# Sliding-window attention and mixture of experts on one core: attention's order written anew, four pairs' softmax sums moved to VectorE

## The chip, the core and the metric

One core of a Trainium2 chip runs the whole program in one launch. The metric is the device time in microseconds (us) of the program; lower is better. Engines are named as in the profile: PE (TensorE matmul), PEld (its weight loads), DVE (VectorE), ACT (ScalarE), POOL (GpSimd), SP (SyncE, which issues most DMAs here).

## What is computed

Attention with a sliding window of 128 and 4 sink positions, on 4 batches of 8 heads of 768 positions of 64 columns, and behind it a top-2 mixture of 8 experts with a hidden width of 1024:

```python
scores = scale * np.matmul(q, k.transpose(0, 1, 3, 2))
scores = np.where(is_sink | in_window, scores, -1e9)
a = np.exp(scores - scores.max(-1)); a = a / (a.sum(-1) + 1e-9)
x = (a @ v)                        # (3072 rows, 512)
noisy = x @ w_gate + log1p(exp(x @ w_noise)) * noise
top2 of noisy per row, weights = softmax over the two
out[row] += weight * relu(x[row] @ w1[e]) @ w2[e]   # for both experts
```

## The kernel before

Attention is cut into 48 steps n (16 groups g of two heads, three steps each; each step holds four blocks of 128 query rows, 528 columns of scores in all). Two steps are a pair m = n // 2. The parts of a step, by the function in the code:

- `qk` (PE, L413): scores of step n into a PSUM tile S. It reads the group's `kq` tile, loaded by SP (`load_kq`, L387, 816 KB).
- `prev` (ACT or DVE, L420/L418), `cur0`, `cur` (DVE, L432, L436), `cur1` (POOL, L440): the scores go to the SBUF ring `cbuf`, masked.
- `mins` (DVE, L443): the maximum of each row. `minus_max` (POOL, L446): its scaled negative, `nb`.
- `exps_sums` (ACT, L457): four exponentials of 132 columns with `nb` as bias, each with an accumulated sum that is read out by a second instruction.
- `sums_e` (POOL, L470) adds 1e-9 to a pair's sums, `sums_i` (DVE, L484) takes reciprocals.
- `ptr` (PE, L502): transposes of the probabilities into a PSUM tile P; `ptr_c` copies it (`CT`), `ptr_m` masks it (`CM`, POOL L518 or DVE L515), `sink_c` copies the sink part.
- `pv` (PE, L528 with `vn` and `CT`, L531 with `dv` and `CM`), where `vn` is loaded by SP (`load_v`, L390, 384 KB) and `dv` is a difference of its blocks made by POOL (`minus`, L320).
- `sinks` (PE, L543), `pv_c` (the result to SBUF, ACT or DVE), `rows` (DVE, L557), and for a batch's rows a write to `x_rows` in HBM (`rows_d`, L562).

Routing of batch b (logits on PE, L742 and L750, then many small steps) is laid between the attention steps of batch b + 1; its matmuls are called `rank` (L856 to L862) and `place` (L956). From `place` follow the row numbers `idg` (DVE, L980), an indirect fetch of rows by POOL (L1028), their scaling (`norm`, DVE, L1080 and L1082) and their transposes on PE (`turn`, L1090). Four tiles are fetched ahead like this, the last of them behind batch 2's routing. The first expert matmuls (`up_ahead`, L1182 to L1184) end this phase; the experts follow.

The order of the work is written out by hand. `Plan.op` numbers every step; the string `ORDER` lists the numbers in the order in which they are issued, and each engine runs its own steps in that order, each waiting for what it reads. `SIDE` says by one digit for each step that may run on either of two engines which one it is. `BANKS` gives the PSUM bank of each tile; S, P and the routing tiles share three of two banks. `GATES` holds the issue of a DMA back until a certain `qk` has run (`42:1`: step 42 waits for `qk(1)`). The steps called `warm` (L374, 17 of them) are matmuls of ones whose result nobody reads; they keep PE at work while it has nothing else. `END` is the point at which each engine is taken to be free when phase two's order is worked out (`Plan.run`).

Of the kernel before, what the change touches and what calls it, by code (L numbers as in the profile page):

```python
# [16 lines left out]
AF = mybir.ActivationFunctionType  # L17
# [3 lines left out]
PR = dict(load_qk=0.0, load_v=24.264, w1=36, pc_pool=0, gap_8=1, dv_pool=4, et=42, cm_pool=8, gap=4, subs=0)  # L21
CAP = 832

# [57 lines left out]
"""  # L81
SIDE = """
00000101100011100111100110100100100010101001000001100110100000110001100101100000010010000010010001100000010110010000
0110000111100100001110010100
"""
BANKS = """
10120121021102012010210201021021012101201002112010102112001211010210210120011202101012102001210120102011201021120012
0012001112010210102102110201201100211120110021002102
# [4 lines left out]
143:2 42:1 44:3 90:7 145:9 189:15 195:12 266:16 268:4 317:10 319:16 387:23 456:18 529:18 533:15 582:20 650:22 652:32  # L93
722:23 801:30 803:31 854:32 856:42 950:47 1012:38 1100:47 1102:44 1106:46 1108:47 1110:45 1112:47 1114:47 1116:39
1125:15 1139:47
"""
END = dict(PE=155.2, ACT=154.0, DVE=155.7, Pool=149.9, SP=160.6, DMA=164.3)
# [221 lines left out]
def minus(eng, out, a, b):  # L319
    eng.tensor_tensor(out, a, b, op=OP.subtract)  # L320
# [34 lines left out]
def attention(tc, plan, cst, sh, kqs, v, vss, xbuf):  # L355
    nc = tc.nc
# [91 lines left out]
    def sub(n, eng):  # L448
        minus(nc.gpsimd if eng == "Pool" else nc.vector, C(n), C(n),
              get("mn", n)[:, :, None].to_broadcast([128, 4, KW]))  # L450
# [8 lines left out]

    def exps_bias(n):  # L460
        for u in range(4):
            nc.scalar.activation(C(n)[:, u], C(n)[:, u], AF.Exp, bias=get("nb", n)[:, u:u + 1], scale=1.0 / math.sqrt(D))

    def exps_each(n):
        for u in range(4):
            nc.scalar.activation(C(n)[:, u], C(n)[:, u], AF.Exp, scale=1.0 / math.sqrt(D),
                                 accum_out=get("sm", n // 2, [128, 2, 4])[:, n % 2, u:u + 1])
# [118 lines left out]
    for g in range(NP):  # L586
# [11 lines left out]
        for jj in range(NJ):  # L598
# [13 lines left out]
            each = bias = m * 7 % 24 >= PR.get("subs", 0)  # L612
            if bias:
                op("Pool", .15, n + .4 + P(g, "sub"), lambda n=n: minus_max(n), r=[("mn", n)], w=[("nb", n)])
                if each:
                    op("ACT", 1.545, n + .4 + P(g, "exps"), lambda n=n: exps_sums(n), r=[("nb", n)], w=[("C", n), ("sm", m, odd)],
                       u=[("sm", m)])
                else:
                    op("ACT", 1.18, n + .4 + P(g, "exps"), lambda n=n: exps_bias(n), r=[("nb", n)], w=[("C", n)])
            else:  # L620
                op("Pool", 1.03, n + .4 + P(g, "sub"), lambda n=n: sub(n, "Pool"), r=[("mn", n)], w=[("C", n)])
                if each:
                    op("ACT", 1.19, n + .4 + P(g, "exps"), lambda n=n: exps_each(n), w=[("C", n), ("sm", m, odd)], u=[("sm", m)])
                else:
                    op("ACT", .53, n + .4 + P(g, "exps"), lambda n=n: exps(n), w=[("C", n)])
# [998 lines left out]
```

## Time and profile before

| | us |
|---|---|
| three runs | 719.23, 721.18, 721.12; median 721.12 |
| profiled execution, its own time | 717.77 |
| its span, first to last instruction | 716.1 |
| PE busy | 703.1 (98%) |
| POOL busy | 386.0 (54%) |
| DVE busy | 420.1 (59%) |
| ACT busy | 308.1 (43%) |

The shares are means over two phases that differ: attention up to 152 us, where all engines are at work, and the experts behind it, where PE is busy nearly throughout and the other engines are not. So the profile is read by stretches.

### The profile page before, as it was taken

Reading aid. Unit: us, or ns where it says so; the run is one execution under the profiler, and the core shown is the slowest. Engines: PE = TensorE matmul, PEld = TensorE weight load, DVE = VectorE, ACT = ScalarE, POOL = GpSimd, SP = SyncE. Lnnn points to the kernel's source line nnn. Section 1 sums busy time; section 2 is a strip of 40 time slices with the busy share of each in tenths; the row PEclk is TensorE's granted clock in tenths of the full one; section 3 lists DMA queues with packets and bytes.
Section 4 is the critical chain, followed back from the end, with each engine's and each line's share of the span. In section 5 each row is a group of like instructions: output and inputs, shape, how many; then the busy total and the mean of one; then the engine's idle time right before and its main releaser. Section 6 shows DMA issues by size and latency. Waiting matters only on the chain.

```text
span 716.1 us, 16960 instructions
## 1 busy us (share of the span) xinstructions
PE 703.1 (98%) x6580; PEld 626.3 (87%) x6580; DVE 420.1 (59%) x1008; ACT 308.1 (43%) x823; POOL 386.0 (54%) x602
## 2 busy tenths in 40 slices
PE   8999999999999999999999999999999999999996
PEld 4878787768899989989999999999999999999994
DVE  7889999988547545553564366436544734473310
ACT  6999999942244233313331343134313421442210
POOL 3647668711466755465556645663567373737012
PEclk9999999999999999999999999999999999999999
DMA  7566777777866616372737364736554560634023
GB/s 231 194 231 193 184 217 225 167 225 204 293 116 196 169 35 166 129 189 52 178 129 174 62 170 145 167 64 177 178 109 92 165 151 26 155 119 78 6 40 45
DMA packets 68467, 104.63 MB, mean 146 GB/s; under 512 B 20112, under 2 KB 41360, under 8 KB 68384
## 3 DMA queue, kind: packets, MB, share of 16 engines
q1 hardware_dynamic: 55104, 75.71, 34.3%
q0 software_dynamic: 13280, 27.81, 20.5%
q8 instruction: 52, 0.85, 0.5%
q14 instruction: 31, 0.25, 0.1%
HBM read 72.79 MB, written 30.70 MB: 145 GB/s over the span
## 4 chain that ended last, share of the span: by engine, by line
PE 86%; DVE 4%; issue 4%; POOL 2%; DMA 2%; ACT 1%; POOLq 0%; DVEq 0%; ACTq 0%
PE H L1182 12%; PE H L1184 12%; PE H L1183 12%; PE Y L1242 8%; PE Y L1241 8%; PE Y L1240 8%; PE Y L1250 4%; PE Y L1251 4%; PE Y L1249 4%; PE D L413 4%; PE D L502 3%; PE X L528 2%; PE X L531 2%; PE X L543 1%; POOL out L1283 1%
## 5 line engine op out<-in xcount | busy, mean ns | idle before, releaser
L1034 POOL DMA_INDIRECT xg<-x_rows,rt_idq x173 | 174.5, 1009 | 62.8 <-issue 46.1
L1182 PE MATMUL H<-skn,w 128*128 128x384 f32 (+4 forms) x508 | 174.0, 343 | 0.0
L1184 PE MATMUL H<-skn,w 128*128 128x384 f32 (+4 forms) x508 | 173.7, 342 | 0.0
L1183 PE MATMUL H<-sqn,w 128*128 128x384 f32 (+4 forms) x508 | 173.2, 341 | 0.0
L1226 ACT ACTIVATE h<-H 128x384 fp32r<-128x384 f32 (+4 forms) x127 | 63.4, 499 | 250.5 <-PE H L1184 244.8
L1231 DVE SCALAR_TENSOR_TENSOR h<-H,h 128x384 fp32r<-128x384 f32 (+4 forms) x127 | 71.5, 563 | 159.8 <-ACT h L1226 159.7
L1283 POOL DMA_INDIRECT out<-y,idx x46 | 80.8, 1756 | 52.2 <-ACT y L1278 41.0
L1183 PEld LDWEIGHTS H<-sqn,w 128*128 128x128 f32 x508 | 95.5, 188 | 5.1 <-DVE sqn L320 0.2
L1182 PEld LDWEIGHTS H<-skn,w 128*128 128x128 f32 x508 | 95.4, 188 | 5.2 <-DVE lt L753 0.3
L1292 POOL COPY spacer<-h 1x1 f32<-1x1 f32 x88 | 25.0, 284 | 133.7 <-ACT h L1226 133.4
L1184 PEld LDWEIGHTS H<-skn,w 128*128 128x128 f32 x508 | 95.3, 188 | 1.8
L457 ACT ACTIVATE cbuf<-cbuf,nb 128x132 f32<-128x132 f32 x192 | 75.1, 402 | 1.8 <-POOL nb L446 0.9
L1104 ACT ACTIVATE skn<-xtn 128x512 fp32r<-128x512 f32 (+2 forms) x46 | 27.6, 605 | 63.8 <-DVE xtn L1095 63.8
L1242 PE MATMUL Y<-w2a,h 128*128 128x512 f32 x136 | 53.9, 396 | 0.0
L1240 PE MATMUL Y<-w2a,h 128*128 128x512 f32 x136 | 53.6, 394 | 0.0
L1241 PE MATMUL Y<-w2a,h 128*128 128x512 f32 x136 | 53.5, 394 | 0.0
L1240 PE MATMUL Y<-w2b,h 128*128 128x512 f32 x136 | 53.5, 393 | 0.0
L1241 PE MATMUL Y<-w2b,h 128*128 128x512 f32 x136 | 53.4, 393 | 0.0
L1242 PE MATMUL Y<-w2b,h 128*128 128x512 f32 x136 | 53.3, 392 | 0.0
L320 DVE TENSOR_TENSOR w<-st,w 128x1024 fp32r<-128x1024 f32 x30 | 36.6, 1222 | 9.1 <-ACT w L1142 9.0
L413 PE MATMUL D<-kq 64*64 64x200 f32 (+3 forms) x832 | 39.4, 319 | 2.1 <-DVE mn L443 2.1
L320 DVE TENSOR_TENSOR sqn<-xtn,skn 128x512 fp32r<-128x512 f32 (+2 forms) x46 | 30.0, 658 | 17.0 <-ACT skn L1104 16.8
(214 smaller groups left out, 1332.3 us busy)
## 6 DMA issues: line engine op xcount, KB each, us to landing
st<-in_w1l SPq DMA_DIRECT2D x32, 512.0 KB
st<-in_w2l SPq DMA_DIRECT2D x32, 512.0 KB
kq<-in_kq SPq DMA_DIRECT2D x15, 816.0 KB
vn<-in_v SPq DMA_DIRECT2D x16, 384.0 KB
x_rows<-xr SPq DMA_DIRECT2D x48, 128.0 KB
out<-zt SPq DMA_DIRECT2D x24, 256.0 KB
y<-y_rows SPq DMA_DIRECT2D x14, 256.0 KB
xg<-x_rows,rt_idq POOLq DMA_INDIRECT x173, 2.8
```

Source lines behind the costliest of these rows:

```text
L320: eng.tensor_tensor(out, a, b, op=OP.subtract)
L413: last = nc.tensor.matmul(x[:, o:o + w], kq(g)[r, 1, j, t], k[:, f:f + w], start=True, stop=True)
L457: nc.scalar.activation(C(n)[:, u], C(n)[:, u], AF.Exp, bias=get("nb", n)[:, u:u + 1], scale=1.0 / math.sqrt(D), accum_out=get("sm", n // 2 ...
L1034: nc.gpsimd.indirect_dma_start(out=x[:, i, :], out_offset=None, in_=xbuf.rearrange("r (q d) -> (r q) d", d=sh.SW), in_offset=bass.Indirect ...
L1182: nc.tensor.matmul(p, w[:, 0], xh, start=(i == 0), stop=False)
L1183: nc.tensor.matmul(p, w[:, 0], xl, start=False, stop=False)
L1184: nc.tensor.matmul(p, w[:, 1], xh, start=False, stop=(i == sh.DM // 128 - 1))
L1231: nc.vector.scalar_tensor_tensor(h[:, width:2 * width], p, 0.0, h[:, :width].bitcast(F32), op0=OP.max, op1=OP.subtract)
L1240: nc.tensor.matmul(p, hh, w[:, 0], start=(f == 0), stop=False)
L1241: nc.tensor.matmul(p, hh, w[:, 1], start=False, stop=False)
L1242: nc.tensor.matmul(p, hl, w[:, 0], start=False, stop=(f == FC - 1))
L1283: d = nc.gpsimd.indirect_dma_start(out=out, out_offset=bass.IndirectOffsetOnAxis(ap=x[:size(e, t), t:t + 1], axis=0), in_=get("y", Y[e, t] ...
```

## The change

For the pairs m = 3, 4, 5 and 7 (steps 6 to 11, 14 and 15) the softmax is done in another way: POOL subtracts the row maxima from the 528 columns (`sub`, in place of `minus_max`), ACT takes one exponential over them (`exps`), and DVE sums them (`sums`, a reduction over 133 columns for each of the four blocks, the last of them holding 1e-9, so that `sums_e` falls away for these pairs). The functions `sub`, `exps` and `sums` stood in the code before and were not used (`subs=0`).

```diff
-PR = dict(load_qk=0.0, load_v=24.264, w1=36, ..., gap=4, subs=0)
+PR = dict(load_qk=0.0, load_v=24.264, w1=36, ..., gap=4)
+SUBS = (3, 4, 5, 7)
...
-END = dict(PE=155.2, ACT=154.0, DVE=155.7, Pool=149.9, SP=160.6, DMA=164.3)
+END = dict(PE=155.2, ACT=154.0, DVE=155.7, Pool=149.9, SP=164.1, DMA=166.1)
...
-            each = bias = m * 7 % 24 >= PR.get("subs", 0)
+            each = m not in SUBS
...
+                op("Pool", 1.03, n + .4 + P(g, "sub"), lambda n=n: sub(n), r=[("mn", n)], w=[("C", n)])
+                op("ACT", .53, n + .4 + P(g, "exps"), lambda n=n: exps(n), w=[("C", n)])
+            op("DVE", 0 if each else .62, n + .8 + P(g, "sums"), None if each else lambda n=n: sums(n), r=[("C", n)],
+               w=[("sm", m, odd)], u=[("sm", m)])
```

`ORDER`, `SIDE`, `BANKS` and `GATES` are new in full. With their numbers replaced by names, this is what they say:

- PE has the same 223 steps. Its changes between kinds of step (scores and transposes, `pv`, sinks, others) are 126 instead of 124. PE's order at the start, before and after:

```
before: warm x7, qk0 qk1 qk2, warm x2, qk3 qk4 qk5, warm x7, ptr0 ptr1 qk7, warm, qk6 pv0 pv1 sinks0 ptr2 ptr3 qk9 ptr4 qk8 pv2
after:  warm x3, qk0 qk1, warm x6, qk2, warm x7, qk3 qk5 qk4, warm, ptr1 qk7 ptr0 qk6 ptr2 pv0 pv1 sinks0 ptr3 qk8 qk9 pv2
```

- At the end of attention, from batch 2's `rank` on:

```
before: qk46 qk47 rank ptr42 pv40 pv41 sinks20 turn turn ptr43 pv42 ptr44 ptr45 pv43 sinks21 ptr46 pv44 pv45 place
after:  qk46 qk47 pv40 rank pv41 ptr42 ptr43 sinks20 turn ptr44 pv42 pv43 sinks21 ptr45 turn pv44 pv45 ptr46 place
both:   place sinks22 ptr47 pv46 proj pv47 sinks23 turn turn proj proj turn up_ahead ... turn up_ahead
```

- POOL's last steps before: `tc1` `ptr_m43` `minus_max47` `dv15` `tc0` `sums_e22` `ga` `ga` fetch; after: `tc1` `dv15` `tc0` `em` `ids` `ga` `ga` fetch, where `tc` are the two products of L946 that `place` reads and `ga` what `idg` reads. DVE made `op1` `tc0` `op0` last ahead of `place`; now `tc0` `tc1` `op1` come earlier and `op0` is last.
- Steps that may run on two engines: ACT takes 37 `prev` instead of 26, 44 `ptr_c` instead of 39, 27 `pv_c` instead of 36, 11 `pcopy` instead of 10; DVE takes 11 `prev` instead of 22, 4 `ptr_c` instead of 9, 21 `pv_c` instead of 12; POOL takes 13 `pcopy` instead of 14.
- SP's loads: `kq` of group 2 now goes ahead of `v` of group 0 (held for `qk0` instead of `qk2`), `v` of group 1 is held for `qk3` instead of `qk7` and goes ahead of `kq` of group 3, `v` of groups 4 and 5 for `qk12` and nothing instead of `qk16`, `v` of group 13 for `qk37` instead of `qk42`, of group 14 for `qk40` instead of `qk47`. Zero writes are spread over attention in another way, and the last rows written (`xrow 11`) come behind four of them at the end.
- With the new `END`, phase two's order is the same on PE, ACT, DVE and POOL; on SP two weight loads now go ahead of two zero writes at its start.

## Rows read from the trace of the kernel before

**Rows 1.** Busy time by stretch: PE (instructions), PEld, DVE, ACT, POOL, clock, DMA share, GB/s.
```profile
4.36:13.88 9.52, 7.46 (x115) 4.83 (x114) 6.31 (x14) 6.38 (x27) 2.07 (x7) 1.00 0.81 265
13.88:137.00 123.12, 122.83 (x3278) 98.93 (x3277) 114.13 (x353) 117.33 (x486) 82.94 (x194) 1.00 0.70 207
137.00:152.04 15.04, 13.04 (x293) 9.98 (x290) 13.25 (x32) 9.54 (x34) 7.49 (x13) 1.00 0.53 122
152.04:185.00 32.96, 32.96 (x183) 26.66 (x184) 24.99 (x90) 9.41 (x15) 6.31 (x12) 1.00 0.85 260
```

**Rows 2.** Timeline of PE, 66 to 68 us: start, duration, instruction.
```profile
66.80 0.61 PE L531 MATMUL X<-CM,dv 128*64 128x128 f32 x8
67.34 0.71 PE L543 MATMUL X<-ps,vr 16*128 16x128 f32 x8
67.98 0.91 PE L413 MATMUL D<-kq 64*64 64x200 f32 x16
```

**Rows 3.** Timeline of PE, from the start to 14 us.
```profile
1.25 3.17 PE L374 MATMUL X<-one 128*128 128x512 bf16 x7 [1.25 <-DVE one L309]
...
10.16 2.16 PE L413 MATMUL D<-kq 64*64 64x132 f32 x52 [2.06 <-DVE mn L443]
...
12.26 1.68 PE L374 MATMUL X<-one 128*128 128x512 bf16 x7
...
13.88 1.16 PE L502 MATMUL D<-idf,cbuf 64*64 64x64 f32 x64
```

**Rows 4.** Waits of PE from 136 to 152 us: total, times, longest.
```profile
PE D L1090 <- DVE xg L1082: 0.6, 1, 0.6
PE D L502 <- ACT CT L420: 0.6, 1, 0.6
PE D L956 <- POOL rt_tc L946: 0.4, 1, 0.4
PE X L528 <- DVE xtn L418: 0.3, 1, 0.3
```

**Rows 5.** Timeline around the last fetch: PE, POOL, PE.
```profile
143.36 0.47 PE L956 MATMUL D<-rt_tc,rt_op 128*128 128x56 f16 x12 [0.41 <-POOL rt_tc L946]
...
141.91 1.40 POOL L946 TENSOR_TENSOR rt_tc<-rt_tc,tok 128x336 f16<-128x336 f16 x1 [1.79 <-DVE rt_tc L943]
...
144.96 1.07 POOL L1028 DMA_INDIRECT xg<-x_rows,idg  x1 [0.79 <-DVE ri L484]
...
149.84 0.66 PE L1090 MATMUL D<-idf,xg 128*128 128x128 f32 x4 [0.61 <-DVE xg L1082]
```

**Rows 6.** Timeline of ACT: one step's four exponentials, first row and next step.
```profile
43.42 0.44 ACT L457 ACTIVATE cbuf<-cbuf,nb 128x132 f32<-128x132 f32 x1
...
44.97 0.40 ACT L746 ACTIVATE lt<-D 128x256 f32<-128x256 f32 x1
```

**Rows 7.** Groups by line up to 165 us: count, busy us, mean ns, idle before.
```profile
L443 DVE TENSOR_REDUCE mn<-cbuf 128x4 f32<-128x528 f32 x48 | 32.6, 686 | 1.0 <-POOL cbuf L440 0.7
L320 POOL TENSOR_TENSOR dv<-vn 128x640 f32<-128x640 f32 x16 | 24.8, 1550 | 4.1 <-DMA vn<-in_v 2.1 <-PE D L413 1.7 <-ACT xtn L420 0.2
L420 ACT ACTIVATE CT<-D 128x512 f32<-128x512 f32 x39 | 23.0, 593 | 2.8 <-DVE mn L443 1.5 <-PE D L502 1.2
L420 ACT ACTIVATE cbuf<-D 128x528 f32<-128x528 f32 (+1 forms) x26 | 14.6, 567 | 4.7 <-PE D L413 4.4
L420 ACT ACTIVATE xtn<-X 128x256 f32<-128x256 f32 x36 | 12.7, 378 | 2.7 <-PE X L543 2.6
L418 DVE COPY cbuf<-D 128x264 f32<-128x264 f32 (+1 forms) x22 | 12.4, 564 | 3.5 <-PE D L413 2.9 <-POOL dv L320 0.5
L446 POOL TENSOR_SCALAR nb<-mn 128x4 f32<-128x4 f32 x48 | 12.3, 257 | 10.0 <-DVE mn L443 7.2 <-DVE rt_tq L930 0.8 <-DVE rt_tv L932 0.7
L418 DVE COPY CT<-D 128x512 f32<-128x512 f32 x9 | 6.2, 684 | 1.0 <-PE D L502 1.0
```

**Rows 8.** Waits from 10 to 152 us that a load ended.
```profile
POOL dv L320 <- DMA vn<-in_v: 2.1, 2, 1.6
```

More of the change, by code (lines that the diff above doesn't have):

```diff
@@ L20 @@
 BIG = 1.0e30
-PR = dict(load_qk=0.0, load_v=24.264, w1=36, pc_pool=0, gap_8=1, dv_pool=4, et=42, cm_pool=8, gap=4, subs=0)
+PR = dict(load_qk=0.0, load_v=24.264, w1=36, pc_pool=0, gap_8=1, dv_pool=4, et=42, cm_pool=8, gap=4)
 CAP = 832
+SUBS = (3, 4, 5, 7)
 CAPS = (800, 832, 800, 800, 800, 768, 768, 768)
@@ L41 @@
 ORDER = """
[39 rows of a table removed]
[41 rows of a table added]
 """
 SIDE = """
-00000101100011100111100110100100100010101001000001100110100000110001100101100000010010000010010001100000010110010000
-0110000111100100001110010100
+00000011100010011100100010110111001000001100000001001100011010000011001000001100011000000000001000000100010010010000
+0111000101100111000101000100
 """
 BANKS = """
-10120121021102012010210201021021012101201002112010102112001211010210210120011202101012102001210120102011201021120012
-0012001112010210102102110201201100211120110021002102
+02010210210110210101201200102100211201021012110210012120101021102012010210012102010121201002110201102012101021101021
+0012001101210210010211001202110002101021100211002102
 """
 GATES = """
-143:2 42:1 44:3 90:7 145:9 189:15 195:12 266:16 268:4 317:10 319:16 387:23 456:18 529:18 533:15 582:20 650:22 652:32
-722:23 801:30 803:31 854:32 856:42 950:47 1012:38 1100:47 1102:44 1106:46 1108:47 1110:45 1112:47 1114:47 1116:39
-1125:15 1139:47
+93:3 149:0 198:12 200:7 276:6 278:12 332:7 405:20 477:15 479:23 611:28 680:24 682:33 757:33 837:28 841:38 895:37 992:40
+1057:36 1148:47 1150:17 1152:36 1154:47 1156:47 1158:45 1162:46 1164:25 1166:11 1173:15 1187:45 1189:46
 """
-END = dict(PE=155.2, ACT=154.0, DVE=155.7, Pool=149.9, SP=160.6, DMA=164.3)
+END = dict(PE=155.2, ACT=154.0, DVE=155.7, Pool=149.9, SP=164.1, DMA=166.1)
 class Plan:
@@ L446, in minus_max, with sub @@
         nc.gpsimd.tensor_scalar(get("nb", n, [128, 4]), get("mn", n), -1.0 / math.sqrt(D), None, op0=OP.mult)
-    def sub(n, eng):
-        minus(nc.gpsimd if eng == "Pool" else nc.vector, C(n), C(n),
-              get("mn", n)[:, :, None].to_broadcast([128, 4, KW]))
+    def sub(n):
+        minus(nc.gpsimd, C(n), C(n), get("mn", n)[:, :, None].to_broadcast([128, 4, KW]))
     def exps(n):
@@ L458, in exps_sums @@
                                  scale=1.0 / math.sqrt(D), accum_out=get("sm", n // 2, [128, 2, 4])[:, n % 2, u:u + 1])
[L460 to L467, printed above, removed]
     def sums_e(m):
@@ L611, in attention @@
             m, odd = divmod(n, 2)
-            each = bias = m * 7 % 24 >= PR.get("subs", 0)
-            if bias:
+            each = m not in SUBS
+            if each:
                 op("Pool", .15, n + .4 + P(g, "sub"), lambda n=n: minus_max(n), r=[("mn", n)], w=[("nb", n)])
[L615 to L619, printed above, removed]
-            else:
[L621 to L625, printed above, removed]
-            if not each:
-                op("DVE", .62, n + .8 + P(g, "sums"), lambda n=n: sums(n), r=[("C", n)], w=[("sm", m, odd)], u=[("sm", m)])
+                op("ACT", 1.545, n + .4 + P(g, "exps"), lambda n=n: exps_sums(n), r=[("nb", n)], w=[("C", n), ("sm", m, odd)],
+                   u=[("sm", m)])
+            else:
+                op("Pool", 1.03, n + .4 + P(g, "sub"), lambda n=n: sub(n), r=[("mn", n)], w=[("C", n)])
+                op("ACT", .53, n + .4 + P(g, "exps"), lambda n=n: exps(n), w=[("C", n)])
+            op("DVE", 0 if each else .62, n + .8 + P(g, "sums"), None if each else lambda n=n: sums(n), r=[("C", n)],
+               w=[("sm", m, odd)], u=[("sm", m)])
             if odd:
@@ L643, in attention @@
             if odd:
-                if each:
-                    op("Pool", .15, n + .6 + P(g, "sums_i"), lambda m=m: sums_e(m), r=[("sm", m, 0), ("sm", m, 1)],
-                       w=[("sm", m)])
+                op("Pool", .15 if each else 0, n + .6 + P(g, "sums_i"), (lambda m=m: sums_e(m)) if each else None,
+                   r=[("sm", m, 0), ("sm", m, 1)], w=[("sm", m)])
                 op("DVE", .19 if n % NJ == 0 else .1, n + .6 + P(g, "sums_i"), lambda m=m: sums_i(m), r=[("sm", m, 0), ("sm", m, 1), ("sm", m)], w=[("rin", m)],
```

80 rows, old and new, of the table ORDER are left out of this document.

## The prediction

> **What bounds the kernel now.** I read the busy times by stretch first, then PE's own timeline, then PE's waits, and only then the groups of the other engines, because a saving counts only where PE would otherwise stand still.
>
> The stretches [rows 1] show three regimes in attention. From 4.36 to 13.88 us PE is busy 7.46 of 9.52 us: the pipeline fills. From 13.88 to 137 it is busy 122.83 of 123.12, so 0.29 us are left. From 137 to 152.04 it is busy 13.04 of 15.04, so 2.0 us are idle. Behind that, the next 33 us have no idle time on PE at all. What the experts take after 152.04 is therefore fixed by PE's own work, and the change can act only through the moment at which the expert matmuls start.
>
> A busy PE can hide waits, since the ends of matmuls are modelled. So I looked at start-to-start distances [rows 2]: eight mask products take 67.34 - 66.80 = 0.54 us, eight sink products 67.98 - 67.34 = 0.64. Steps of the same kind and follower repeat these within 0.03 us through the stretch, whether the operands had been ready for long or had just come. That is an engine running through a queue of ready work, not one that is fed piece by piece. ACT is busy 117.33 and DVE 114.13 of the 123.12 us [rows 1], close to full as well, but neither makes PE wait in that stretch.
>
> **The softmax of four pairs.** Eight steps change. On ACT a step's four exponentials with their sums take 44.97 - 43.42 = 1.55 us [rows 6]; one exponential over 528 columns is priced by the copy of 528 or 264 columns, 0.57 us [rows 7]. That is 8 x (1.55 - 0.57) = 7.8 us less on ACT. In return ACT takes 11 more `prev` at 0.567 and 5 more `ptr_c` at 0.593 and gives up 9 `pv_c` at 0.378 [rows 7]: 6.2 + 3.0 - 3.4 = 5.8 more. ACT's net is 2.0 us less. DVE gets 8 sums at 0.69 (the row maxima read 528 columns in 686 ns), loses 11 copies at 0.564 and 5 at 0.684, and takes 9 of the result at about ACT's price of 0.378 [rows 7]: 5.5 - 6.2 - 3.4 + 3.4 = -0.7 us. POOL gets 8 subtractions of 528 columns. It has no such row; `dv`, the same kind over 640 columns, takes 1.55 us [rows 7], and scaled by columns that is 1.28 us. It loses 8 `minus_max` at 0.257. POOL's net is 10.2 - 2.1 = 8.1 us more, less four small adds.
>
> None of this is work of PE. In the middle stretch it is worth between -0.29 us (all idle time of PE there goes) and whatever new wait it makes. Its cover is the distance in PE's order between a step's scores and its transposes. If a subtraction made a transpose late, each such step would cost up to the subtraction's own 1.28 us, 8 x 1.28 = 10.2 us as the outer end. For a step by itself the path hardly changes: 0.257 + 1.55 = 1.81 us from maximum to probabilities before, 1.28 + 0.57 = 1.85 after. So I take +0.1 us for the middle stretch, near the lower end, and keep the upper for a rival.
>
> **PE's own order.** Two more changes between kinds of step. A group of eight mask products takes 0.54 us when another kind follows [rows 2]; the like without a change of kind cannot be below zero, so two changes cost 0 to 1.1 us. I take 0.2.
>
> **The start.** Before, six scores and nine warm steps lie between the first scores and the first transposes at 13.88 [rows 3]. The second group's scores began at 10.16 after a wait of 2.06 us, which is the landing of its load, and the six scores without that wait need about 3.1 + 2.1 us. The new order has 13 warm steps ahead of `qk3`. At 1.68 / 7 = 0.24 us each [rows 3] that is 3.1 us, so `qk3` can start at 4.36 + 3.1 + 3.1 = 10.6 us, just behind the load. Three scores (2.1) and one warm step (0.3) lead to the first transposes at 13.0, 0.9 us earlier than 13.88. Against this, `v` of group 0 now lies behind 816 KB of `kq` for group 2. At 265 GB/s [rows 1] these take 3.1 us, and POOL's `dv0` (1.55), the masks and `minus_max3` stand behind that load in POOL's queue. The first `pv` comes late in the new order (behind `ptr2`), which covers most of it. I give back 0.5 us (0 to 1.5). Start: -0.4 us, from -0.9 to +0.6.
>
> **The end of attention.** PE's waits there [rows 4] are 0.6 for the last fetched rows, 0.6 for a copy by ACT, 0.4 for the products that `place` reads, 0.3 for a copied result: 1.9 of the 2.0 idle us. From `place` to the transposes of the fetched rows are 149.84 - 143.36 = 6.48 us [rows 5], and PE's work between them is the same in both orders, about 6.48 - 0.61 - 0.3 = 5.6 us. The fetch, its scaling and that last wait stay. What can go is the 0.41 us ahead of `place`: `tc0` is made earlier on DVE, and POOL's second product no longer runs against DVE's `op`. That product took 1.40 us [rows 5]. POOL also has `ga` ready sooner, so I take 0.3 us off the 144.96 - 143.36 = 1.6 us between `place` and the fetch. End: -0.7 us, from -1.9 (all listed waits go) to +1.0 (`op0`, now last on DVE ahead of `place`, comes late by about one such step).
>
> **Transfers.** Before, POOL waited twice for a `v` load, 2.1 us in all [rows 8], without a wait of PE behind it. Groups 4, 5, 13 and 14 are now released earlier. In the profiled execution that is worth nothing; in an execution whose loads land a microsecond later such a wait would reach PE. I take -0.3 us, from -1.5 to 0. The spread zero writes and the late `xrow 11` lie on SP ahead of fetches that need batch 3's routing, far behind; the two weight loads ahead of two zero writes move by less than a microsecond. Both at nothing: if that cover were gone, PE's first 33 us of experts without an idle moment [rows 1] would show it.
>
> **Sum.** +0.1 + 0.2 - 0.4 - 0.7 - 0.3 = -1.1 us. The profiled execution took 717.77 us (span 716.1, 1.7 us around it) and would become 716.7. It was 3.35 us below the median of the runs, 721.12. Carried over to the median: 720.0 us, say 719.9.
>
> **The rivals.** *ACT is the bound, hidden behind modelled ends.* For: ACT's 95% in the middle stretch. Against: the constant distances of PE. It would give 721.1 - 2.0 (ACT's net) - 0.7 (the end) - 0.6 (load room and the middle's idle time) = 717.8 us. [...]
>
> *POOL becomes the bound, slower.* From the first `sub` to the last are some 25 us in which POOL is already 82.94 / 123.12 = 67% busy [rows 1], 17 of 25 us; 8.1 us more fill it. Then its queue decides, in which `dv`, the masks and the subtractions wait for one another in order. It decides once a subtraction takes longer than the room left, 8 / 8 = 1 us above `minus_max`; at 1.28, with an order written for the 1.03 that the code counts for it, each is 0.25 late, and 8 x 0.25 = 2 us. A product of POOL that ran beside DVE's `op` took 1.40 us [rows 5]; should subtractions be drawn out like it, the price grows to some 3.3. Between 2.0 and 3.3, less what the end gains: 723.5 us. Against it: all 16 rows of `dv` keep their 1550 ns [rows 7] beside a DVE that is busy 93% of the time, and the new order has more distance between scores and transposes in some of these steps.
>
> [...]
>
> *The order does not do what it says:* the steps are moved but PE's waits stay where they are; that is within the forecast's own range.
>
> **Chances.** Forecast (719.9, own range 718.3 to 721.6) 0.48; ACT bound (717.8) 0.14; half rate at the start (721.8) 0.22; POOL bound (723.5) 0.16. A measurement of this kernel tells about 0.3%, 2.2 us, from no change: faster means below 718.96, slower above 723.28. Faster: the ACT rival and a third of the forecast, 0.30. Slower: the POOL rival and a little of the slow start, 0.18. Same: 0.52. Range: 717.1 to 723.6.
>
> **What would show it.** Right: PE idle below 1.5 us in its last 15 us of attention, `place` without a wait, the first transposes near 13 us, and the middle stretch with under 0.6 us of idle PE. ACT's busy share should fall without PE's start of the experts (152.04) moving by more than two microseconds. Wrong: waits of transposes for POOL's `sub` or for ACT's `exps` between 20 and 45 us; a subtraction above 1.4 us; first transposes behind 14.5 us; or an expert start before 150, which would say that ACT had been the bound.

## The result, and the profile after

Six runs each: 724.94 us (724.11 to 726.63) after, 720.62 (718.29 to 722.73) before; ratio 1.0066, 95% interval 1.0043 to 1.0090. The forecast was 719.9 with a range that ended at 723.6: slower came true, at 0.18. The interval lies wholly above 1. The profiled execution after took 724.11 us, 6.3 more than that of before; its span, 722.5 us, is 6.4 longer.

Busy time by stretch after (columns as in [rows 1]); the cuts are the first scores, the first transposes, 140 us, and the start of the experts' first loop.

```profile
4.10:14.54 10.44, 10.44 (x118) 5.63 (x119) 5.56 (x14) 5.10 (x21) 1.53 (x7) 1.00 0.72 248
14.54:140.00 125.46, 123.56 (x3295) 99.57 (x3294) 117.12 (x355) 113.98 (x440) 89.89 (x187) 1.00 0.72 210
140.00:159.12 19.12, 16.64 (x287) 12.74 (x287) 17.45 (x46) 12.77 (x44) 8.28 (x16) 1.00 0.44 122
159.12:192.00 32.88, 32.88 (x182) 26.87 (x183) 22.61 (x83) 7.60 (x13) 8.65 (x14) 1.00 0.82 248
```

ACT's share of the middle stretch fell from 95% [rows 1] to 113.98 / 125.46 = 91%, POOL's rose from 67 to 72%. PE's idle time there is 125.46 - 123.56 = 1.90 us where before had 0.29, and the stretch from 140 us on has 2.48, of which one wait takes 1.50. PE's timeline at the start (answers to [rows 3]):

```profile
1.25 1.46 PE L376 MATMUL X<-one 128*128 128x512 bf16 x3 [1.25 <-DVE one L311]
4.10 2.73 PE L415 MATMUL D<-kq 64*64 64x132 f32 x36 [1.39 <-DMA kq<-in_kq]
6.76 2.74 PE L376 MATMUL X<-one 128*128 128x512 bf16 x6
...
10.51 1.68 PE L376 MATMUL X<-one 128*128 128x512 bf16 x7
...
14.54 0.67 PE L494 MATMUL D<-idf,cbuf 64*64 64x64 f32 x29
```

Six warm steps behind the first scores take 6.76 to 9.44, 0.45 each, the next seven 0.24: PE has stood still for 1.39 us ahead of the first scores, and the granted clock reads 1.00 from 4.10 to 14.54, over the slow steps and the fast ones alike. The first transposes come at 14.54, not at 13.0.

PE's timeline at the hand-over from attention to the experts, after:

```profile
154.31 0.48 PE L1167 MATMUL D<-skn,w 128*128 128x512 f32 x1
...
157.21 0.40 PE L1169 MATMUL D<-skn,w 128*128 128x512 f32 x1
159.12 0.47 PE L1167 MATMUL H<-skn,w 128*128 128x512 f32 x1 [1.50 <-DVE rt_ab L806]
```

DVE's timeline beside it:

```profile
158.28 0.69 DVE L1216 SCALAR_TENSOR_TENSOR h<-D,h 128x512 fp32r<-128x512 f32 x1 [0.22 <-ACT h L1211]
158.88 0.20 DVE L806 SCALAR_TENSOR_TENSOR rt_ab<-lg 128x48 f32<-128x48 f32 x1
```

And PE's timeline at the same place in the kernel before:

```profile
154.78 0.39 PE L1184 MATMUL D<-skn,w 128*128 128x512 f32 x1
155.06 0.50 PE L1182 MATMUL H<-skn,w 128*128 128x512 f32 x1
```

`up_ahead` is the same work in both, yet from its start to the first matmul into H are 159.12 - 154.31 = 4.81 us after and 155.06 - 151.91 = 3.15 before. The label names `rt_ab`, DVE's last event before the start. But that step reads and writes SBUF tiles alone (`lg`, `rt_ab`), and H lies in PSUM. L1216 just ahead of it, which reads the hidden rows of `up_ahead` in PSUM, ends at 158.97. Before, the weight load of H's first matmul waited 0.32 us for another reader, L753, which reads a tile of the routing's logits and ends at 155.00:

```profile
154.58 0.42 DVE L753 TENSOR_TENSOR lt<-D,ri 128x256 f32<-128x256 f32 x1 [0.19 <-PE D L750]
```

The softmax of four pairs (groups by line up to 165 us; columns as in [rows 7]):

```profile
L322 POOL TENSOR_TENSOR cbuf<-cbuf,mn 128x528 f32<-128x528 f32 x8 | 8.5, 1069 | 3.3 <-DVE mn L445 3.1 <-ACT cbuf L422 0.2
L465 DVE TENSOR_REDUCE sm<-cbuf 128x4 f32<-128x532 f32 x8 | 5.5, 692 | 0.8 <-ACT cbuf L454 0.8
L454 ACT ACTIVATE cbuf<-cbuf 128x528 f32<-128x528 f32 x8 | 5.2, 648 | 1.2 <-POOL cbuf L322 1.2
```

And PE's list of waits from the first transposes to the experts (answers to [rows 4]; total, times, longest). No wait for `xg`, for `rt_tc` or for a load is in it, and none for `sub`, `exps` or `sums`.

```profile
PE H L1167 <- DVE rt_ab L806: 1.5, 1, 1.5
PE X L520 <- ACT CT L422: 0.5, 1, 0.5
PE D L494 <- ACT CT L422: 0.4, 1, 0.4
PE D L494 <- DVE rt_ro L909: 0.3, 1, 0.3
...
PE D L415 <- issue: 0.2, 1, 0.2
```

### The profile page after: what moved, and what is told of

It is laid out like the page before. It is cut to its first block, busy times and chain, and to the rows that moved or that the text cites. A ratio compares the mean times of both kernels' runs of the same rounds, so it can differ in the third digit from the quotient of the medians.

```text
span 722.5 us, 16912 instructions
## 1 busy us (share of the span) xinstructions
PE 706.5 (98%) x6580; PEld 627.6 (87%) x6580; DVE 423.4 (59%) x1009; ACT 305.3 (42%) x775; POOL 399.0 (55%) x597
## 4 chain that ended last, share of the span: by engine, by line
PE 82%; DVE 6%; issue 5%; POOL 3%; DMA 2%; ACT 1%; SPq 1%; POOLq 0%; DVEq 0%; ACTq 0%
PE H L1167 12%; PE H L1169 12%; PE H L1168 12%; PE Y L1227 8%; PE Y L1225 8%; PE Y L1226 8%; PE Y L1234 3%; PE Y L1235 3%; PE Y L1236 3%; PE D L415 3%; PE D L494 2%; PE X L520 2%; DMA st<-in_w1l 1%; PE X L523 1%; PE X L535 1%
## 5 line engine op out<-in xcount | busy, mean ns | idle before, releaser
L1019 POOL DMA_INDIRECT xg<-x_rows,rt_idq x173 | 178.7, 1033 | 63.2 <-issue 47.4
L1216 DVE SCALAR_TENSOR_TENSOR h<-H,h 128x384 fp32r<-128x384 f32 (+4 forms) x127 | 71.6, 564 | 161.4 <-ACT h L1211 148.3
L1277 POOL COPY spacer<-h 1x1 f32<-1x1 f32 x88 | 26.6, 302 | 129.5 <-ACT h L1211 127.9
L458 ACT ACTIVATE cbuf<-cbuf,nb 128x132 f32<-128x132 f32 x160 | 62.7, 404 | 2.3 <-POOL nb L448 2.2
```

The costliest lines, as they stand in the source:

```text
L1019: nc.gpsimd.indirect_dma_start(out=x[:, i, :], out_offset=None, in_=xbuf.rearrange("r (q d) -> (r q) d", d=sh.SW), in_offset=bass.Indirect ...
L1216: nc.vector.scalar_tensor_tensor(h[:, width:2 * width], p, 0.0, h[:, :width].bitcast(F32), op0=OP.max, op1=OP.subtract)
```

## The experiments

Two executions can differ by 5 us at the start of the experts while PE's work is the same, so each trace is read by the same four marks. The table has, worked out from the starts of PE's rows: first transposes; from there to `place`; from `place` to `up_ahead`; from `up_ahead` to the first matmul into H. The ratio to before is that of all runs, against runs of before made beside them; new means the changed kernel's order.

| kernel | first transposes | to `place` | to `up_ahead` | to H | ratio |
|---|---|---|---|---|---|
| before, profiled | 13.88 | 129.48 | 8.55 | 3.15 | 1 |
| before, e7 | 12.68 | 135.67 | 8.56 | 3.14 | |
| before, e8 | 12.45 | 133.55 | 8.55 | 3.15 | |
| after | 14.54 | 131.80 | 7.97 | 4.81 | 1.0066 |
| e1: new, PSUM place | 13.49 | 135.42 | 7.97 | 3.18 | 1.0038 [1.0017, 1.0059] |
| e2: new, start | 12.69 | 137.03 | 7.97 | 4.80 | 1.0032 [1.0009, 1.0055] |
| e3: new, small steps | 13.59 | 135.28 | 7.97 | 4.80 | 1.0064 [1.0042, 1.0086] |
| e4: all three | 12.20 | 133.51 | 7.98 | 3.19 | 1.0021 [1.0003, 1.0038] |
| e10: e1 and e2 | 12.61 | 134.24 | 7.96 | 3.18 | 1.0019 [1.0003, 1.0035] |

**One place in PSUM (e1).** My theory: each tile's place follows from the order in which places are first asked for, and the experts' first H gets the one that attention asked for first. In `BANKS` the hidden rows of `up_ahead` have place 2 in both kernels; the first scores, `qk0`, have place 0 before and place 2 after. So in the new order the first H lies where `up_ahead`'s last hidden rows lie, and waits until DVE (L1216) has read them; before, it lay where logits of the routing had been. The edit asks for Y ahead of H:

```diff
-    plan.rings.update(y=4, h=9, X=2, H=2, w2b=2)
+    plan.rings.update(y=4, h=9, X=2, H=2, w2b=2, Y=4)
...
+    plan.get("Y", 0, [128, sh.DM], F32, "ps")
```

> The changed kernel with one difference: in the experts' phase a Y tile is given its place in PSUM before the H tiles, so that the first H lies in the place of a tile that the routing's logits used, and not in the place of the last attention tile, which holds the hidden rows of `up_ahead`. My theory: the 1.50 us that PE stands still at 159.12 in the changed kernel, behind DVE, is a wait for that place (H may not be written before `up_l` has read the tile). Then the first H starts within 0.5 us of the end of `up_ahead`, PE has no wait over 0.3 us between 154 and 165, and the ratio to the kernel before falls by 1.66 / 720.6 from 1.0066 to about 1.0043. Rival: PE would have to wait there anyway, for the hidden rows that DVE makes at 158.28 to 158.97 (or for weights); then the wait of 1.5 us comes back within the next 5 us under another name, and the ratio stays at 1.0066.

PE's timeline of e1 at the hand-over:

```profile
159.78 0.40 PE L1169 MATMUL D<-skn,w 128*128 128x512 f32 x1
160.06 0.51 PE L1167 MATMUL H<-skn,w 128*128 128x512 f32 x1
```

The wait is gone: H starts 0.78 us ahead of L1216 (160.84), and its weight load waits 0.32 us for the logits' reader, as before. The distance is that of the kernel before in every trace with this edit (e1, e4, e9, e10), and 4.79 to 4.81 in every trace with the new `BANKS` and without it (after, e2, e3, and e5 below). So it was the place; how a tile comes by it is read from the code, not measured. The ratio is 0.0028 (2.0 us) lower than that of the changed kernel, but the two intervals overlap: 1.65 us by the traces is the better figure.

**Warm steps ahead of the first load (e2).** Four warm steps go ahead of the first scores, so that PE runs from 1.25 us on:

```diff
+MOVES = (([39, 19, 13, 25], 17),)   # four warm steps, put behind the third
-plan.replay(tc, [int(x) for x in ORDER.split()], ...)
+plan.replay(tc, shifted(ORDER), ...)   # shifted puts each list's steps behind the step named after it
```

> The changed kernel with one difference: four of the warm steps that PE runs behind the first scores are put ahead of them, so that seven run before the first load lands, as in the kernel before. My theory: the six warm steps at 0.45 us and the slow scores behind them were the lower rate, and with seven warm steps ahead the rate rises about as early as before; the first transposes start at 13.9 us or earlier (14.54 in the changed kernel) and the whole kernel is 0.5 to 1.0 us shorter: ratio about 1.0055. Rival one: the load of the third score step sets the start, not the rate: first transposes stay at 14.5. Rival two: the start is faster, but what follows is bound by DVE and POOL, and by 60 us the gain is gone: ratio 1.0066.

PE's timeline of e2 at the start:

```profile
1.25 3.17 PE L376 MATMUL X<-one 128*128 128x512 bf16 x7 [1.25 <-DVE one L311]
...
6.82 0.60 PE L376 MATMUL X<-one 128*128 128x512 bf16 x2
...
12.69 0.69 PE L494 MATMUL D<-idf,cbuf 64*64 64x64 f32 x32
```

The two warm steps behind the first scores now take 0.60 us together, as they do before (0.61), and the first transposes come 1.85 us earlier. Over the traces of the new order: 13.9 on the mean with three ahead (14.54, 13.49, 13.59 and, of e5 below, 13.93), 12.5 with seven (12.69, 12.20, 12.61 and, of runs below, 12.19, 13.26, 12.27, 12.05). So the edit is worth 1.4 us at this mark. Before, with seven, has 13.88, 12.68, 12.45 and, below, 12.89 and 12.18: 12.8 on the mean. Two more traces of the old order are later, 15.50 (e14, unchanged up to here) and 15.58 (e6): there PE waited 2.10 and 1.90 us for the second scores, and these then took 3.37 and 3.83 us against 2.16. Seven warm steps do not rule a slow start out. The ratio fell by 0.0034 (2.5 us) from after to e2 and by 0.0019 (1.4 us) from e1 to e10; both pairs of intervals overlap.

**DVE's small steps beside POOL's long ones (e3).** A theory that fell. After, three small steps of DVE that take some 0.2 us elsewhere lasted to the end of a `dv` of POOL that ran beside them: 0.95, 1.43 and 1.55 us. e3 moves four routing steps of DVE and two steps of POOL away from each other; e4 adds e1 and e2.

```diff
+MOVES = (([736, 734, 735, 737], 714), ([1183], 843), ([897], 910))
```

> The changed kernel with only three groups of steps put elsewhere in the order: on DVE the four small steps of the routing of batch 1 at 103 us come behind the two mask products that follow them; on POOL a rest of a weight that ran at 102.70 comes at about 116, and `dv` of group 13 comes one step later. My theory: in the changed kernel a small step of DVE that falls on a long step of POOL takes until that one ends (1.43 us instead of 0.15 at 103.72, 1.55 instead of 0.19 at 125.96), so DVE is 2 to 3 us late between 103 and 113, and PE waits in 104 to 124 (1.7 us by start-to-start distances) come from that. Then the stretched steps go, DVE's long small steps sum to under 2 us (4.6 in the changed kernel), the experts start 1 to 2 us earlier, and the ratio is about 1.0045. Rival: PE's waits there come from POOL's own queue (three fetches between 118 and 123 ahead of the small sums on the scores); then the small steps are short, and the waits at 121.9 and 124.1 stay, and the ratio with them.

> The three differences together. If the three losses are separate, 1.66 + 0.66 + 1.0 to 1.7 us go: ratio 1.0012 to 1.002, and what is left over the kernel before is the wait for fetched rows at 228 us (2.0 us in the profiled execution), if that comes again. If they hide one another (each gain is waited away further on), the ratio stays above 1.004.

Two such steps are left (0.96 us each), the time stayed at 1.0064, and e4 equals e10 (1.0021 and 1.0019), which has no such moves. DVE lost time there, but the kernel's time did not hang on it.

**Which half of the change (e5, e6).** The engines' new order with the old order of SP and its gates, and the reverse:

```diff
 e5: ORDER, SIDE, BANKS of after; SP's steps and GATES of before
 e6: ORDER, SIDE, BANKS of before; SP's steps and GATES of after
```

> The changed kernel with SP's steps (all loads, row writes and zero writes) in the order and with the releases of the kernel before; only where a step must come earlier for its reader is it put there (two steps). The four engines keep the new order. My theory, formed on the last four traces: PE reads its own instructions from memory in blocks of 16 KB (some 256 instructions), which share the DMA engines with the data. The new order packs its loads closer, the blocks land later than they did before (mean 2.4 to 3.0 us behind the point at which they are asked for, against 1.8 before; in 6 to 11 of 27 blocks PE reaches the first instruction within 1.8 us of its landing, against 1 of 27 before), and PE's waits marked `issue` (0.2 to 1.3 us each, 2 to 4 us in some executions) are that. Then with the old transfers the blocks are early again: under 3 such blocks of 27, no `issue` wait over 0.3 us in attention, first matmul of the experts 1 to 3 us earlier than in the changed kernel, ratio 1.002 to 1.005. Rival: the steps' order on the engines makes the waits, and old transfers come too late for it (waits of PE and POOL for `kq` and `vn`): ratio 1.0066 or more.

> The reverse: the kernel before, with SP's steps in the order and with the releases of the changed kernel. By my theory the instruction blocks come later (6 or more of 27 within 1.8 us of their first reader), `issue` waits appear, and the kernel is 1 to 3 us slower than before: ratio 1.0015 to 1.004. By the rival (the engines' order makes the waits) the ratio is 0.999 to 1.001, or it falls, since the loads come earlier.

e5 took 748.72 us (1.0384), e6 732.07 (1.0147). PE's longest waits in attention, of e5:

```profile
PE X L522 <- ACT xtn L424: 4.0, 2, 3.8
PE D L737 <- ACT lt L733: 3.5, 2, 3.2
```

And of e6:

```profile
PE X L528 <- DMA vn<-in_v: 3.3, 1, 3.3
PE X L531 <- POOL CM L518: 1.6, 1, 1.6
```

Either half alone is worse than both kernels, by more than either expectation gave; e5's ratio is on the side of its rival, though its longest waits are for ACT and not for loads. An order and its transfers are one thing; no time can be credited to a half. Two readings of the traces can: the hand-over to H takes 4.79 us in e5 and 3.14 in e6, so it goes with the engines' order and its `BANKS`; and e6, the old order with the new transfers, has 3.9 us of the `issue` waits that come next, e5 1.1.

**Two more traces of before (e7, e8).** The unchanged kernel, profiled twice more, since its first trace had no wait for a load.

> The kernel before, unchanged, for a second trace of it: the first one shown ran in 717.8 us and had no `issue` wait of PE in attention, while the median of all its runs is 720.8. If late instruction blocks are a matter of chance in both kernels, this trace has `issue` waits too and takes 720 to 722 us; if the old transfers leave the blocks room, there are at most 2 late blocks of 27, and the difference to 717.8 lies elsewhere (waits for loads, for fetched rows).

> The kernel before once more, for a third trace, with the same two readings as the one ahead of it.

PE's waits in attention, of e7:

```profile
PE D L413 <- DMA kq<-in_kq: 2.0, 2, 1.1
PE D L413 <- issue: 1.8, 1, 1.8
PE D L413 <- DVE cbuf L436: 1.0, 1, 1.0
```

And of e8:

```profile
PE D L413 <- DMA kq<-in_kq: 2.7, 3, 1.1
```

So the waits that the change takes away were there in two of three executions, 2 to 3 us of `qk` for loads of `kq`. None appears in a trace of the new order with its own transfers, behind its start. But `issue` waits do, in which PE waits for nothing that the profile shows. I read them as waits for PE's own instructions, for which the page lists a DMA queue beside those of the data. The page of the changed kernel, its busy times and the queue that carries them (packets, MB, share):

```profile
PE 706.5 (98%) x6580; PEld 627.6 (87%) x6580; DVE 423.4 (59%) x1009; ACT 305.3 (42%) x775; POOL 399.0 (55%) x597
...
q8 instruction: 52, 0.85, 0.5%
```

PE's 6580 matmuls and 6580 weight loads are 253 to each of the 52 blocks, and 0.85 MB are 16 KB to each. In e1, from 53 to 54.4 us, data alone move (DMA queues):

```profile
q1 hardware_dynamic: 66, 0.35, 60.3%
```

From 54.4 to 55.4 us one block of instructions comes:

```profile
q8 instruction: 1, 0.02, 5.5%
```

And PE, which had stood still for 1.31 us, goes on at 56.70:

```profile
56.70 0.57 PE L415 MATMUL D<-kq 64*64 64x200 f32 x8 [1.31 <-issue]
```

The traces bear the reading out. In all 18, `issue` held PE up 38 times between its first transposes and the experts (0.15 us or more each), and every one of these waits ended 1.2 to 1.7 us behind the landing of a block on q8. Waits behind the same block end at the same instruction in every trace in which they occur, seven of them behind the fifth block.

PE's `issue` waits in attention came to 0, 1.8 and 0 us in the three traces of before, and to 0.2 (after), 2.6 (e1), 3.8 (e2), 2.5 (e3), 1.2 (e4) and 1.9 (e10) in the new order. I counted the blocks whose first instruction ran within 1.8 us of its landing (which instruction is a block's first is an estimate, counted on from those at which the waits ended): 1, 5 and 5 of 27 before; 6, 6, 11, 9, 8 and 9 in the new order. So late blocks are not the new order's alone, but more frequent in it. Most blocks came without a wait of PE: 38 waits in 18 traces, with some 27 blocks in each.

**Taking the new waits away (e9, e10).** e10 is e1 and e2 together. e9 also releases the `kq` loads of groups 8 to 13 singly, with `vn` loads between them, so that no long burst forms:

```diff
 e9, SP:  kq8 (gate qk20) vn6 kq9 (qk23) vn7 kq10 (qk25) vn8 kq11 (qk28) vn9 kq12 (qk31) ...
```

> The changed kernel with seven warm steps ahead of the first scores and the Y tile placed ahead of the H tiles (both as tried before), and with its loads spread: between 50 and 105 us the `kq` loads of groups 8 to 13 are released one at a time, each 4 to 6 us before PE can need it in full (they had 6 to 16 us of room), `vn` loads go between them, and two zero writes and the blank rows go behind them. My theory (blocks of PE's instructions wait behind data that is queued on the DMA engines): the blocks that are asked for between 50 and 105 us land within 3.5 us (up to 6.6 us before), no `issue` wait over 0.3 us is left there, and the kernel is 0.5 to 1.5 us faster than the one with the same start and tiles and the loads as they were (e10): ratio 0.9995 to 1.001. Rival: `issue` waits come from PE's own pace (transposes that run through their instructions faster than any block can come): they stay, and the ratio is that of e10.

> The changed kernel with the seven warm steps ahead and the Y tile ahead of the H tiles, nothing else: the base for e9 and e11. As e4 without its moves in DVE's and POOL's order, which I now think were worth nothing: ratio 1.001 to 1.003. If the moves counted, it is above 1.0035.

e10: 720.96 us, 1.0019 [1.0003, 1.0035]. e9: 1.0026 [1.0003, 1.0049]. Its `issue` waits fell from 1.9 to 0.4 us and its late blocks from 9 to 5, yet its waits for engines rose from 2.2 to 4.4, and the gain that was expected did not come. In this trace the wait changed its kind.

**The same in the old order (e12, e16).** Loads of `kq` 6 and 14 (e12), or 6 alone (e16), released earlier in the kernel before:

```diff
+MOVES = (([385, 386], 1119), ([948, 949], 804))   # e12; e16 has the first alone
```

> The kernel before with two loads earlier on SP's queue: `kq` of group 6 ahead of the gate's and a weight's load, `kq` of group 14 ahead of the routing's row writes and the blank rows. In its second and third trace PE waited 1.07 to 1.10 us at 43 to 45 us for the first and 0.89 to 0.94 us at 119 to 121 us for the second. Theory: in most executions of the kernel before these two waits are there, they are what the change took away, and without them it takes 1.5 to 2.0 us less: ratio 0.997 to 0.998, better than both kernels. Rival: the time comes back at the next load or as `issue` waits: 0.999 to 1.001.

> The kernel before with one load earlier on SP's queue: `kq` of group 6 ahead of the gate's and a weight's load. In e12 the same edit took away the wait of 1.1 us at 43 us, and what that kernel lost came behind its other edit (the fetch at 117 us landed late behind row writes that had been put behind a load). So here the ratio should be 0.9985 (1.1 us less). If the load's wait comes back elsewhere, it is 1.000.

PE's timeline at the wait that took the load's place, of e12:

```profile
124.59 1.12 PE L413 MATMUL D<-kq 64*64 64x132 f32 x20 [2.95 <-DVE cbuf L436]
```

And of e16:

```profile
39.52 0.44 PE L528 MATMUL X<-CT,vn 128*64 128x128 f32 x4 [1.60 <-issue]
```

e12 took 722.80 us (1.0040 [1.0019, 1.0060]): DVE stood 2.94 us for fetched rows whose writes, behind the earlier load in SP's queue, took SP 6.34 us. e16: 1.0015 [0.9990, 1.0040]. Both expectations missed: in the old order too, an earlier load bought nothing that these runs can show.

**What the four pairs' softmax is worth (e11).** e10 with `SUBS = ()`, the sums of these pairs back on ACT, and their four `sums_e` on POOL put where they are needed:

```diff
-SUBS = (3, 4, 5, 7)
+SUBS = ()
-MOVES = (([39, 19, 13, 25], 17),)
+MOVES = (([39, 19, 13, 25], 17), ([179], 195), ([221], 181), ([254], 305), ([351], 314))
```

> The kernel of e10 with the softmax of all pairs in the old form (sums by ACT's exponentials; POOL scales the maxima; no subtraction and no sums on DVE), in the new order. By my theory the four pairs' sums are worth nothing either way: POOL's subtractions took 1.07 us each and PE waited for none of them. Ratio that of e10 within 0.0015. Rival one: POOL's 6.6 us more between 22 and 45 us delay what follows: this kernel is 1 to 2 us faster than e10. Rival two: ACT's 7.8 us less did help: this one is 1 us or more slower, with waits of PE for the exponentials between 25 and 50 us.

e11 took 726.23 us, 1.0083 [1.0060, 1.0107], by the ratios 4.6 us above e10: the second rival, not my expectation. PE's waits in attention:

```profile
PE D L415 <- ACT CT L422: 2.6, 2, 1.4
PE D L727 <- ACT cbuf L458: 1.2, 1, 1.2
PE D L494 <- ACT CT L422: 1.0, 1, 1.0
```

These waits lie between 26 and 55 us, where the four pairs are. The new order gave ACT 11 `prev` and 5 `ptr_c` more; without the sums' relief ACT holds PE up there. The relief pays for the order, and together they gain nothing.

**Is another engine the bound? (e13, e14, e15)** e13 is e10, e14 is before, with ACT's work cut from step 16 (about 45 us) on: the maxima's subtraction and the sums are left out; e15 is e13 with DVE's maxima and POOL's `minus_max` left out too.

```diff
 e13, e14:  +        if n >= 16: return exps(n)        # one exponential, maximum not subtracted
            +        if m >= 8: return memset(sm, 200.0)   # shortened; in sums_e
 e15:       +        if n >= 16: return                # mins, minus_max
```

> The kernel of e10 (new order, seven warm steps ahead, Y tile first) with less work on ACT: from step 16 on, the four exponentials of a step with their sums are one exponential over all columns, without maximum, and the sums are set to a constant. This leaves out the maxima's subtraction and the sums for two thirds of the steps; the order is the same. It takes some 28 x 1.0 us off ACT between 45 and 145 us. If PE's own stream holds attention (my reading in the prediction), the first matmul of the experts comes at most 1.5 us earlier than in e10 (157.99), and PE's waits that remain are those for DVE and POOL. If ACT holds it, the experts start 3 us earlier or more.

> The same cut in the kernel before (maxima's subtraction and sums left out from step 16 on). The prediction's rival `ACT is the bound` says that ACT, busy 95% in the middle of attention, set the pace of the kernel before: then the experts start 3 us earlier or more than in its three traces (155.06, 157.70, 160.05). If PE's stream set it, the start is within the range of these three, and PE's busy share of the stretch stays as it was.

> As e13, and from step 16 on DVE's row maxima and POOL's scaling of them are left out too (32 x 0.68 us less on DVE). If DVE is what held attention in the new order once loads are early, this starts the experts 1.5 us or more ahead of e13; if PE's stream did, within 0.7 us of it. `issue` waits tell the third reading: if instruction blocks hold PE, they grow in both, since PE would otherwise be faster.

Busy time from 45 to 145 us (columns as above) of e10:

```profile
45.00:145.00 100.00, 97.37 (x2486) 77.72 (x2488) 93.62 (x299) 92.03 (x369) 70.17 (x154) 1.00 0.74 212
```

Of e13:

```profile
45.00:145.00 100.00, 97.21 (x2544) 78.73 (x2543) 95.95 (x300) 64.68 (x155) 69.73 (x158) 1.00 0.75 215
```

Of e15:

```profile
45.00:145.00 100.00, 98.32 (x2510) 79.25 (x2502) 77.79 (x268) 64.32 (x154) 61.90 (x124) 0.98 0.75 207
```

ACT's work fell by 27 us in this stretch, and e13 came to 0.9996 [0.9974, 1.0019], 0.0023 below e10; e14 to 0.9977 [0.9952, 1.0002]: about 1.6 us in either kernel, which the intervals hardly tell from nothing. Another 18 us off DVE gave nothing: 1.0024 [0.9997, 1.0050]. The first H came at 155.57 us in e13, 159.63 in e14 and 157.19 in e15, against 157.99 in e10; e13's 2.4 us fall between the two marks of its expectation. So from 45 us on PE's own stream sets attention's time, to within some 2 us; the small waits that break it differ from trace to trace. Ahead of 45 us these cuts say nothing, and e11 shows that ACT has little room there.

## Why the prediction was wrong

**What held.** From 45 us on PE is the bound of attention: the cuts of ACT and DVE show it (27 us less on ACT gave 1.6), and there the rival of a hidden ACT bound is false. Ahead of 45 us, where the four pairs lie, it was not tested in the old order. The end: -0.7 was forecast, 0.41 ahead of `place` and 0.3 behind it. From `place` to `up_ahead` the three traces of before take 8.55 or 8.56, those of the new order with the four pairs and all the work from 7.96 to 7.98: -0.58. The fetch goes 147.41 - 146.34 = 1.07 us behind `place` instead of 1.6, a gain of 0.5 where 0.3 was forecast, so the wait of 0.61 for the last fetched rows, which the forecast kept, is gone. The 0.41 us ahead of `place` are gone too, and count in the column before. The softmax: sums 0.692 us (0.69 forecast), subtractions 1.069 (1.28), exponentials 0.648 (0.57), and no wait of PE for any, so the rival of a POOL bound is false (its 723.5 also lies above the middle of its own terms, 721.1 + 2.65 - 0.7 = 723.1, with 2.65 midway between 2.0 and 3.3). Of the 0.18 for slower most was this rival's, so that chance was borne out by other causes.

**The start: "-0.4 us, from -0.9 to +0.6".** A mis-sized term. It priced 13 warm steps at 0.24 us; the six behind PE's pause ran at 0.45, and at 0.30 and 0.32 in e1 and e3, which begin alike. The mean start moved by 13.87 - 12.82 = +1.05 us (by less if e14's 15.50 is counted with before), and the mend gave 1.4 us by the traces. The chance of 0.22 was for a half rate at the start, priced at 721.8 us. No run shows another clock there, nor the 1.9 us that this is above the forecast; the runs showed 0.45 us for a warm step against 0.24 at a granted clock of 1.00. So it was right in kind and too large in size, and the sign written down for it, first transposes behind 14.5 us, came (14.54). [rows 3] of a single trace also misled: a later load made before's start late, 13.88 where four other traces of that start have 12.2 to 12.9, though a fifth has 15.5.

**"What the experts take after 152.04 is therefore fixed by PE's own work, and the change can act only through the moment at which the expert matmuls start."** This step failed outright. A stretch without idle time says nothing of what frees its first operand. The new `BANKS` put the first H onto a tile in use: +1.65 us at the hand-over. No term of the sum and no rival had it.

**Transfers: "-0.3 us, from -1.5 to 0".** The waits for loads went, as the step said, and they were larger than it thought: 2.0 and 2.7 us in e7 and e8. But the gain was not kept. The new order shows waits of PE for its own instructions instead, and where these were thinned out (e9) engines were late instead. That the nearer loads delay the instruction blocks is argued from e1, e6 and e9, a trace each; it is not shown.

**The middle stretch: "+0.1" and "0.2".** From the first transposes to `place`, before has 129.5, 135.7 and 133.6 us (mean 132.9), the new order 131.8 to 137.0 (mean of six 134.5). That is +1.6, but the scatter is larger. With the start at +1.05, the end at -0.58 and the hand-over at +1.65 the four sum to +3.7, against 724.94 - 720.62 = 4.3 measured. With a scatter of some 6 us in one of its terms, that agreement proves little. What does not rest on it: e10, which mends the start and the hand-over, takes the ratio from 1.0066 to 1.0019, 3.4 us of it, and the two intervals do not overlap.

**The base.** The sum was made on a trace with no wait for a load or for instructions, 3.35 us below the median; what the change removes could not be seen in it.

**Open.** With both mends the new order is still at 1.0019 [1.0003, 1.0035], 0.2 to 2.5 us over before. I can't assign that to one cause: `issue` waits are the likeliest by their count, but e9, which removed most of them, gained nothing. No version here beats both kernels.

## What to carry to other kernels

When a new order changes the sequence in which buffers are first asked for, list which place each tile gets and who reads it last, above all at a border between phases. Keep the engine that sets the end at work from its first instruction; here warm steps behind a pause cost up to twice their price (0.45 us against 0.24). And a wait removed from a stream that is nearly full can return as another (here as 2.95 us for DVE in e12 and as 1.60 us of `issue` in e16): ask what the same transfers hold up, instructions among them, and look at more than one trace before pricing waits of a microsecond.

## What the runs showed of the hardware

Instructions came over a DMA queue of their own (q8: 52 blocks of 16 KB, 253 of PE's matmuls and weight loads to each). PE's `issue` waits, up to 1.8 us at a time (e7), ended 1.2 to 1.7 us behind the landing of such a block, in e1 behind one that came after 1.4 us in which data alone moved.

Three small steps of DVE that read two operands from SBUF, started while POOL ran a `dv` on SBUF (0.95, 1.43 and 1.55 us), ended within 0.06 us of it. DVE's timeline after:

```profile
103.53 0.16 DVE L915 TENSOR_SCALAR rt_tq<-rt_g 128x12 int32<-128x12 int32 x1
103.72 1.43 DVE L917 SCALAR_TENSOR_TENSOR rt_tv<-rt_tq,rt_vl 128x12 f32<-128x12 int32 x1
```

POOL's timeline beside it:

```profile
103.56 1.56 POOL L322 TENSOR_TENSOR dv<-vn 128x640 f32<-128x640 f32 x1
105.09 0.20 POOL L855 TENSOR_TENSOR z<-z 128x6 f32<-128x6 f32 x1
```

Twelve columns took 1.43 us; in e3, which moves it away from that `dv`, the four runs of L917 took 0.13 to 0.17. 105.12 is the end of `dv`, 105.15 that of the small step; `dv` itself kept its length (1.56 us here, 1.56 to 1.60 in all 16). One operand showed the like: L916, which reads one tile (128x12), took 0.49 us at 102.97, up to 103.46, beside a difference made by POOL that ended at 103.43, and 0.17 elsewhere.
